# Bringing a layer's results back from features to token rows: TensorE transposes in place of 32x32 transposes and DMA moves

## The chip, the core and the metric

The kernel runs on one core of a Trainium2 chip. The metric is the device time of one execution in microseconds (us); of the kernel before, the median of three runs is 629.09 us.

## The reference

A linear attention without a softmax is followed by a two-level mixture of experts. Each of 4608 tokens (8 batches of 576) has 512 features (8 heads of 64).

```python
kv = np.einsum('bhsd,bhse->bhde', k, v)
out = np.einsum('bhsd,bhde->bhse', q, kv)
rms = np.sqrt(np.mean(out * out, axis=-1, keepdims=True) + 1e-06)
x = out / rms * g_norm            # then heads side by side: (4608, 512)
# each token: best of 4 groups, then best of that group's 4 experts, with softmax weights g_w, e_w
h = np.maximum(x[tokens] @ w1[g, e], 0.0)      # 512 -> 1024
out[tokens] = (g_w * e_w)[:, None] * (h @ w2[g, e])   # 1024 -> 512
```

## The kernel before

**Stages.** The first part (to about 150 us) computes the attention, the norms and the routing, writes each token's row with its factors into a DRAM scratch `scr`, and sorts the tokens by expert. Then the sixteen experts are worked off from the fullest to the emptiest. The list `CAPS` (line 22) gives each rank a fixed number of token places, 384 down to 256; what does not fit goes to an overflow loop at the end. Rank 0 has two of its three blocks done in the first part; its last block of 128 tokens is done at the start of the expert stage. Ranks 1 to 15 are the loop at line 1376.

**Precision.** A float32 operand is split into a high part in a rounded format (`whi`, `xh`, `hh`; ScalarE, lines 242, 1266, 280) and the rest (`wlo`, `xl`, `hl`; VectorE, lines 243, 1267, 281). A product is then three matmuls, high by high, high by rest and rest by high (`three`, lines 306, 307, 311).

**One rank r of the loop, of capacity `cap`.** Layer 1 runs over the eight chunks f of the hidden features: four times three matmuls into a bank `ps`, then ReLU and split into `hh` and `hl`. Layer 2 (`layer2_by_feature`, ranks 1 to 14) runs over the four chunks d of 128 output features: eight times three matmuls into one of three banks `psy`, with features in partitions and the rank's tokens side by side. Rank 15 uses `layer2_by_token`, which gives token rows at once. Besides, in layer 1 the weights of layer 2 are split by quarters (`split_piece`), and in layer 2 those of the next rank's layer 1; that is done by `side`, which also turns and splits the next rank's inputs.

**How inputs are turned.** The tokens' rows are gathered from `scr` (GpSimd, line 249) into `xg`, scaled by GpSimd, and written to a second scratch `xd` (`put_x`, line 1248). `get_x` (line 1254) reads them back as `xq`, so that a 32x32 transpose on VectorE (`turn_x`, line 1260) gives `xt` with features in partitions.

**How results go back.** Before the change VectorE transposes each `psy` bank in 32x32 squares into `yq` (line 1303, one buffer), and `move_y` (line 1274) then puts the squares in place with sixteen DMAs per rank on SP's queue, from `yq` to `yo`. `scatter_rows` (line 253) sends the rows of `yo`, up to 128 at a time, to the output on GpSimd's queue. Since the squares mix the column order, the weights of layer 2 are split in a permuted order (lines 236 to 238), each quarter in two instructions on each engine.

**The clears.** `yq` is written for a multiple of 32 tokens, so the banks are read past `cap`; line 1359 therefore clears part of each `psy` bank, after the first inputs are split and before the last block of rank 0 uses the banks.

**What sets the order.** In the expert stage the order of instructions on each engine is the order of the code, and each engine and queue works in order. SP's queue issues the weight loads (1 MB each, `load_next`, line 209), `put_x`, `get_x` and the moves. Weight tiles share a ring of twelve buffers, so a load waits until the split has read the tile it replaces.

Of the kernel before, what the change touches and what calls it, by code (L numbers as in the profile page):

```python
# [9 lines left out]
F32 = mybir.dt.float32  # L10
# [4 lines left out]
ALU = mybir.AluOpType  # L15
# [6 lines left out]
CAPS = [384, 364, 354, 330, 326, 312, 302, 300, 292, 290, 284, 274, 268, 264, 260, 256]  # L22
# [33 lines left out]
def tile_linattn_moe(ctx: ExitStack, tc: tile.TileContext, qm, qt, k, v, router, w1, w2, out):  # L56
    nc = tc.nc
    P = 128
    B, H, S, D = BATCH, HEADS, SEQ, HEAD_DIM
    NTOK, DM = out.shape  # L60
# [14 lines left out]
    KC = DM // P  # L75
# [8 lines left out]
    RW = DM + H  # L84
# [138 lines left out]
        return parts[0:2], parts[2:4], load  # L223

    def quarter(w, p):
        part = w[p // 2]
        if part[1] is None:  # L230
            for i, nm in ((1, "whi"), (2, "wlo")):
                part[i] = big.tile(list(part[0].shape), F32R, name=nm, tag="w8")
        if part[0].shape[1] == KC:
            n = part[0].shape[2] // 2
            return [[x[:, :, p % 2 * n:(p % 2 + 1) * n] for x in part]]
        src = w[p % 2][0].rearrange("p f (a c i) -> p a f c i", a=2, i=32)
        dst = [x.rearrange("p f (c a i) -> p a f c i", c=2, i=32) for x in part[1:]]
        return [[src[:, a, :, p // 2 * 2:p // 2 * 2 + 2]] + [x[:, p % 2 * 2 + a] for x in dst] for a in range(2)]

    def split_piece(w, p):  # L240
        for x, hi, lo in quarter(w, p):
            nc.scalar.copy(out=hi, in_=x)  # L242
            nc.vector.tensor_tensor(out=lo, in0=x, in1=hi.bitcast(F32), op=ALU.subtract)  # L243

    def blocks(cap):
        return [(j, min(P, cap - j * P)) for j in range((cap + P - 1) // P)]
# [892 lines left out]
    with ExitStack() as ph:  # L1139
# [75 lines left out]
                yield  # L1215
            nc.sync.dma_start(ovt, tab)


        psys = [ps_q.tile([P, 512], F32, name=f"psy{i}", tag=f"psy{i}") for i in range(3)]

        def next_psy():
# [3 lines left out]

        def moves(cap):

            part = [slice(32 * i, 32 * i + 32) for i in range(4)]  # L1230
            return [(a, s_, part[a], part[s_], len(range(s_, (cap + 31) // 32, 4)))
                    for k in range(4) for s_ in range(4) for a in [(s_ + k) % 4]]

        def gather(r):
            xg = mp.tile([P, 3, RW], F32, name="xg")
# [10 lines left out]
        def put_x(r, g):  # L1246
            for j, rows in blocks(CAPS[r] + -CAPS[r] % 32):
                nc.sync.dma_start(xd[r % 2][j * P:j * P + rows, :], g[0][0:rows, j, 0:DM])

        def get_x(r):  # L1250
            n = (CAPS[r] + 31) // 32
            xq = mp.tile([P, 12, P], F32, name="xq", bufs=1)
            for a in range(4):
                nc.sync.dma_start(xq[32 * a:32 * a + 32, 0:n, :],
                                  xd[r % 2][0:32 * n, a * P:(a + 1) * P].rearrange("(b i) f -> i b f", i=32))
            return xq, mp.tile([P, KC, 384], F32, name="xt", bufs=1)

        def turn_x(r, xq, xt, c):
# [8 lines left out]
            nc.vector.scalar_tensor_tensor(out=xl, in0=x, scalar=g2[:, 0:1], in1=xh.bitcast(F32), op0=ALU.mult,  # L1267
                                           op1=ALU.subtract)

        def move_y(r, yq):  # L1270
            yo = mp.tile([P, 3 * DM], F32, name="yo3", tag="yo3").rearrange("p (j f) -> p j f", j=3)
            pq = yq.rearrange("p (j s) f -> p j s f", s=4)
            for a, s_, pa, ps_, n in moves(CAPS[r]):
                nc.sync.dma_start(yo[ps_, 0:n, a * P:(a + 1) * P], pq[pa, 0:n, s_, :])  # L1274
            return [(yo[:, j], rows, gidx[:, r, j:j + 1]) for j, rows in blocks(CAPS[r])]

        def layer2_by_token(r, w2, hh, hl, side):
            n = 0
            for j, rows in blocks(CAPS[r]):
                yo = mp.tile([P, DM], F32, name="yo", bufs=2)  # L1280
                js = slice(j * P, j * P + rows)
                for hf in range(2):
                    side(n, 2 * len(blocks(CAPS[r])), 0)
                    ps = next_psy()
                    o = ps[0:rows, 0:DM // 2]
                    layer2_half(o, w2, hf, hh[:, :, js], hl[:, :, js])
                    nc.scalar.copy(out=by_quarter(yo)[0:rows, :, 2 * hf:2 * hf + 2], in_=by_chunk(o))
                    side(n, 2 * len(blocks(CAPS[r])), 1)
                    n += 1
                scatter_rows(yo, rows, gidx[:, r, j:j + 1])  # L1290

        def layer2_by_feature(r, w2, hh, hl, side):
            cap = CAPS[r]
            n = (cap + 31) // 32
            yq = mp.tile([P, 12, P], F32, name="yq", bufs=1)
            for d in range(KC):
                side(d, KC, 0)
                ps = next_psy()
                cs = slice((d % 2) * P, (d % 2 + 1) * P)
                _, wh, wl = w2[d // 2]  # L1300
                three(ps[:, 0:cap], FC, lambda c: wh[:, c, cs], lambda c: wl[:, c, cs], lambda c: hh[:, c, 0:cap],
                      lambda c: hl[:, c, 0:cap])
                nc.vector.transpose(out=yq[:, 0:n, 32 * d:32 * d + 32],  # L1303
                                    in_=ps[:, 0:32 * n].rearrange("p (b i) -> p b i", i=32))
                side(d, KC, 1)
            return r, yq

        ph.enter_context(tc.manual_schedule(engines={mybir.EngineType.PE, mybir.EngineType.Activation,
                                                     mybir.EngineType.DVE, mybir.EngineType.Pool, SP}))

        w1c, w2c = st["ws"][0:2], st["ws"][2:4]
        xT = mp.tile([P, KC, P], F32, name="xT", bufs=1)
        hr = mp.tile([P, 12, P], F32, name="hr", tag="yq", bufs=1).rearrange("p c t -> p (c t)")
        xr, xs = (mp.tile([P, 3 * DM], F32, name=nm, tag="yo3")[:, 0:n] for nm, n in (("xr", RW), ("xs", DM)))
        gather_rows(xr, P, gidx[:, 0, 2:3])
        cur = gather(1)
        w1n, w2n, load_next = weight_loads(eidx[0:1, 1:2])
# [37 lines left out]
        for c in range(KC):  # L1355
            turn_x(1, xq, xt, c)
            split_x(1, cur, xt, c)
        for x in psys:
            nc.vector.memset(x[:, DM // 2:384], 0.0)
        yo = mp.tile([P, DM], F32, name="yo", bufs=2)  # L1360
        for hf in range(2):
            ps = next_psy()
            o = ps[:, 0:DM // 2]
# [7 lines left out]
            load_next(i)  # L1371
        w1_at = {0: 2, 1: 3}
        w2_at = {2: 0, 4: 1, 5: 2, 7: 3}
        todo, results = None, []
        tables = overflow_tables()
        for r in range(1, NE):
            cap = CAPS[r]
            _, xh, xl = cur
            hh = mp.tile([P, FC, 384], F32R, name="hh", bufs=1)
            hl = mp.tile([P, FC, 384], F32R, name="hl", tag="hl", bufs=1)  # L1380
            if nxt:
                xq, xt = get_x(r + 1)
            if todo:
                results = move_y(*todo)
            for f in range(FC):
                if f in w1_at:
                    split_piece(w1c, w1_at[f])
                if f in w2_at:
                    split_piece(w2c, w2_at[f])
                ps = ps_h.tile([P, 512], F32, name="ps")  # L1390
                layer1(ps[:, 0:cap], w1c, f, xh[:, :, 0:cap], xl[:, :, 0:cap])
                split_h(hh[:, f, 0:cap], hl[:, f, 0:cap], ps[:, 0:cap])
                if r > 1:
                    next(tables, None)
                    next(tables, None)
                if f == 0:
                    nxt2 = gather(r + 2) if r + 2 < NE else None
                if nxt2 and f == 1:
                    scale(r + 2, nxt2)
                    put_x(r + 2, nxt2)  # L1400
                if nxt and f in (3, 5):
                    load_next((f + 1) // 2)
                if f >= 5 and results:
                    scatter_rows(*results.pop(0))
                if f == FC - 1 and r + 1 == NE:
                    nc.gpsimd.drain()
# [142 lines left out]
```

## Time and profile before

| | |
|---|---|
| runs | 629.09, 622.66, 629.69 us; median 629.09 |
| the profiled execution | 625.29 us, span 623.6 us |
| mean granted TensorE clock | 0.954 |
| busy | TensorE 90%, weight loads 84%, VectorE 60%, ScalarE 43%, GpSimd 34% |
| DMA | 156.70 MB, mean 251 GB/s |
| HBM | read 117.74 MB, written 29.31 MB |

A profile is one execution. Busy time is the share of the span in which an engine works at something. In the view of waits, "PE psy L306 <- DVE yq L1303" means that TensorE's matmuls into `psy`, line 306, stood until VectorE's write of `yq`, line 1303, was done. In a timeline the brackets give the idle time just before an instruction and what ended it. In a table of windows the granted clock is the share of full speed that TensorE was given in that stretch.

### The profile page before, as it was taken

What the parts mean: (1) busy time and instruction counts of PE and PEld (TensorE: products, weight loads), DVE (VectorE), ACT (ScalarE), POOL (GpSimd) and SP (SyncE); (2) the same over time, 40 slices, a digit from 0 to 9 for tenths busy, and PEclk for the clock granted to TensorE, in tenths of its full rate; (3) what the DMA queues carried; (4) which work ended last, traced back from release to release, by engine and by line L of the source; (5) the groups of instructions that cost most, each with busy time, mean ns of one, the idle gap of its engine ahead of it and who ended that gap; (6) DMA issues with size and microseconds to landing.
All of it is one profiled execution on the core that took longest, in us unless ns stands there. A gap on an engine that the chain in (4) does not pass through costs nothing.

```text
span 623.6 us, 13421 instructions
## 1 busy us (share of the span) xinstructions
PE 562.0 (90%) x5181; PEld 521.1 (84%) x5199; DVE 375.3 (60%) x786; ACT 267.2 (43%) x534; POOL 210.3 (34%) x281
## 2 busy tenths in 40 slices
PE   8888869999499999999999998979898979898895
PEld 4666757587189999999999997979898979798895
DVE  4235895862527686777677674657566565658470
ACT  0355645612225344544455453534353435345360
POOL 4032323245226235243144343334334243411103
PEclk9898999999889999999999999979998979798999
DMA  8999995648867769596959595969687777859541
GB/s 297 388 410 359 379 376 190 227 164 263 284 200 253 214 190 313 165 344 172 309 148 353 160 336 183 306 195 286 207 281 261 216 277 204 312 145 354 128 136 68
DMA packets 76788, 156.70 MB, mean 251 GB/s; under 512 B 10194, under 2 KB 49442, under 8 KB 65714
## 3 DMA queue, kind: packets, MB, share of 16 engines
q1 hardware_dynamic: 68752, 133.66, 66.3%
q0 software_dynamic: 7824, 22.11, 10.0%
q8 instruction: 42, 0.69, 0.4%
q10 hardware_dynamic: 146, 0.04, 0.1%
q14 instruction: 24, 0.20, 0.1%
HBM read 117.74 MB, written 29.31 MB: 236 GB/s over the span
## 4 chain that ended last, share of the span: by engine, by line
DMA 37%; PE 36%; SPq 14%; DVE 7%; issue 5%; ACT 1%; POOL 0%; POOLq 0%; DVEq 0%
DMA xq<-xd 20%; SPq L1274 12%; DMA wr<-in_w_dram 7%; PE warm L368 4%; DMA yo<-yq 3%; PE ps L311 3%; PE ps L307 3%; PE ps L306 3%; PE psy L311 3%; PE psy L307 3%; PE ops L521 3%; PE psy L306 3%; PE l L295 2%; DVE wlo L243 2%; PE kps L474 2%
## 5 line engine op out<-in xcount | busy, mean ns | idle before, releaser
L243 DVE TENSOR_TENSOR wlo<-wr,whi 128x1024 fp32r<-128x1024 f32 (+1 forms) x180 | 156.2, 895 | 36.6 <-ACT whi L242 34.4
L306 PE MATMUL psy<-hh,whi 128*128 128x364 f32 (+13 forms) x448 | 141.3, 315 | 22.4 <-DVE yq L1303 22.4
L307 PE MATMUL ps<-xl,whi 128*128 128x364 f32 (+14 forms) x480 | 144.2, 300 | 1.3 <-DVE xl L1267 1.3
L306 PE MATMUL ps<-xh,whi 128*128 128x364 f32 (+14 forms) x480 | 144.1, 300 | 0.4 <-DVE hl L281 0.3
L311 PE MATMUL ps<-xh,wlo 128*128 128x364 f32 (+14 forms) x480 | 144.2, 300 | 0.0
L307 PE MATMUL psy<-hl,whi 128*128 128x364 f32 (+13 forms) x448 | 140.3, 313 | 0.0
L311 PE MATMUL psy<-hh,wlo 128*128 128x364 f32 (+13 forms) x448 | 140.2, 313 | 0.0
L242 ACT CAST whi<-wr 128x1024 fp32r<-128x1024 f32 (+1 forms) x180 | 129.8, 757 | 19.5 <-DMA wr<-in_w_dram 19.5
L253 POOL DMA_INDIRECT out_dram<-yo,gall x45 | 47.9, 1064 | 204.4 <-DMA xd<-xg 99.8
L306 PEld LDWEIGHTS psy<-hh,whi 128*128 128x128 f32 x448 | 89.8, 201 | 24.2 <-DVE yq L1303 24.2
L280 ACT ACTIVATE hh<-ps 128x364 fp32r<-128x364 f32 (+14 forms) x120 | 49.8, 419 | 99.4 <-PE ps L311 97.2
L307 PEld LDWEIGHTS ps<-xl,whi 128*128 128x128 f32 x480 | 90.5, 189 | 1.8 <-DVE xl L1267 1.8
L306 PEld LDWEIGHTS ps<-xh,whi 128*128 128x128 f32 x480 | 90.9, 189 | 0.8 <-DVE hl L281 0.8
L277 POOL TENSOR_TENSOR xg<-xg 128x256 f32<-128x256 f32 x82 | 59.9, 755 | 93.2 <-DMA xg<-scr,gall 93.1
L311 PEld LDWEIGHTS ps<-xh,wlo 128*128 128x128 f32 x480 | 90.6, 189 | 0.0
L307 PEld LDWEIGHTS psy<-hl,whi 128*128 128x128 f32 x448 | 89.9, 201 | 0.0
L311 PEld LDWEIGHTS psy<-hh,wlo 128*128 128x128 f32 x448 | 89.8, 200 | 0.0
L1266 ACT ACTIVATE xh<-xt,rw 128x364 fp32r<-128x364 f32 (+14 forms) x60 | 32.6, 543 | 118.3 <-DVE xt L1260 105.3
L281 DVE SCALAR_TENSOR_TENSOR hl<-ps,hh 128x364 fp32r<-128x364 f32 (+14 forms) x120 | 54.8, 463 | 39.5 <-ACT hh L280 36.4
L1303 DVE STREAM_TRANSPOSE yq<-psy 128x320 f32<-128x320 f32 (+3 forms) x56 | 28.4, 508 | 80.1 <-DMA yo<-yq 62.9
L249 POOL DMA_INDIRECT xg<-scr,gall x44 | 57.3, 1302 | 13.3 <-issue 13.1
L368 PE MATMUL warm<-wide_b,ones_b 128*128 128x512 bf16 x124 | 37.0, 428 | 4.1 <-POOL wide_b L102 2.2
(255 smaller groups left out, 588.3 us busy)
## 6 DMA issues: line engine op xcount, KB each, us to landing
wr<-in_w_dram SPq DMA_DIRECT2D x64, 1024.0 KB
scr<-xo SPq DMA_DIRECT2D x36, 256.0 KB
m_q<-in_qm_dram SPq DMA_DIRECT2D x8, 1024.0 KB
xd<-xg SPq DMA_DIRECT2D x32, 256.0 KB
m_k<-in_k_dram SPq DMA_DIRECT2D x7, 1024.0 KB
m_v<-in_v_dram SPq DMA_DIRECT2D x7, 1024.0 KB
yo<-yq SPq DMA_DIRECT2D x116, 48.0 KB
yo<-yq SPq DMA_DIRECT2D x108, 32.0 KB
```

The lines of the kernel that those rows point to most:

```text
L242: nc.scalar.copy(out=hi, in_=x)
L243: nc.vector.tensor_tensor(out=lo, in0=x, in1=hi.bitcast(F32), op=ALU.subtract)
L249: return nc.gpsimd.indirect_dma_start(out=xg[0:rows, 0:RW], out_offset=None, in_=src, in_offset=bass.IndirectOffsetOnAxis(ap=idx[0:rows, : ...
L253: sc = nc.gpsimd.indirect_dma_start(out=out, out_offset=bass.IndirectOffsetOnAxis(ap=idx[0:rows, :], axis=0), in_=yo[0:rows, :], in_offset ...
L277: eng.tensor_tensor(out=out_[:, hs], in0=x[:, hs], in1=factors(xg)[:, h], op=ALU.mult)
L280: nc.scalar.activation(out=hh, in_=ps, func=AF.Relu)
L281: nc.vector.scalar_tensor_tensor(out=hl, in0=ps, scalar=0.0, in1=hh.bitcast(F32), op0=ALU.max, op1=ALU.subtract)
L306: nc.tensor.matmul(ps, lhsT=stat_h(c), rhs=mov_h(c), start=(c == 0), stop=False)
L307: nc.tensor.matmul(ps, lhsT=stat_h(c), rhs=mov_l(c), start=False, stop=False)
L311: nc.tensor.matmul(ps, lhsT=stat_l(d), rhs=mov_h(d), start=False, stop=(d == n - 1))
L368: nc.tensor.matmul(st["warm"], lhsT=ones_b, rhs=wide_b, start=True, stop=True)
L1274: nc.sync.dma_start(yo[ps_, 0:n, a * P:(a + 1) * P], pq[pa, 0:n, s_, :])
```

## The change

Inputs still take the way through `xd`. Results no longer pass through `yq` and the moves: ScalarE copies each `psy` bank to `yt` with its features in partitions (one buffer, as `yq` was); in the next rank's layer 1, after the chunks f = 1, 2 and 3, `back` transposes one block of 128 tokens each with four TensorE instructions into a bank `tp`, VectorE copies the bank to `yo`, and the rows are scattered. Ranks 1 to 14 have three blocks each. `yo` has four buffers of one block in place of two of three. The permuted split of the layer-2 weights becomes a plain one, with one instruction per quarter and engine, and a quarter now comes from one half of the weights where it came from both in turn. The clears are gone. `put_x` moves from f = 1 to f = 4, behind one weight load.

```diff
     def quarter(w, p):
...
-        if part[0].shape[1] == KC:
-            n = part[0].shape[2] // 2
-            return [[x[:, :, p % 2 * n:(p % 2 + 1) * n] for x in part]]
-        src = w[p % 2][0].rearrange("p f (a c i) -> p a f c i", a=2, i=32)
-        dst = [x.rearrange("p f (c a i) -> p a f c i", c=2, i=32) for x in part[1:]]
-        return [[src[:, a, :, p // 2 * 2:p // 2 * 2 + 2]] + [x[:, p % 2 * 2 + a] for x in dst] for a in range(2)]
+        n = part[0].shape[2] // 2
+        return [x[:, :, p % 2 * n:(p % 2 + 1) * n] for x in part]
...
-        def move_y(r, yq):
-            yo = mp.tile([P, 3 * DM], F32, name="yo3", tag="yo3").rearrange("p (j f) -> p j f", j=3)
-            pq = yq.rearrange("p (j s) f -> p j s f", s=4)
-            for a, s_, pa, ps_, n in moves(CAPS[r]):
-                nc.sync.dma_start(yo[ps_, 0:n, a * P:(a + 1) * P], pq[pa, 0:n, s_, :])
-            return [(yo[:, j], rows, gidx[:, r, j:j + 1]) for j, rows in blocks(CAPS[r])]
+        def back(r, yt, j, rows):
+            tp = ps_t.tile([P, 512], F32, name="tp2", tag="pst")
+            for d in range(KC):
+                nc.tensor.transpose(tp[0:rows, d * P:(d + 1) * P], yt[:, d, j * P:j * P + rows], ident)
+            yo = mp.tile([P, DM], F32, name="yo", bufs=4)
+            nc.vector.tensor_copy(out=yo[0:rows], in_=tp[0:rows, :])
+            scatter_rows(yo, rows, gidx[:, r, j:j + 1])
...
         def layer2_by_token(r, w2, hh, hl, side):
...
-                    nc.scalar.copy(out=by_quarter(yo)[0:rows, :, 2 * hf:2 * hf + 2], in_=by_chunk(o))
+                    nc.scalar.copy(out=yo[0:rows, hf * (DM // 2):(hf + 1) * (DM // 2)], in_=o)
...
         def layer2_by_feature(r, w2, hh, hl, side):
...
-            yq = mp.tile([P, 12, P], F32, name="yq", bufs=1)
+            yt = mp.tile([P, KC, 384], F32, name="yt", bufs=1)
...
-                nc.vector.transpose(out=yq[:, 0:n, 32 * d:32 * d + 32],
-                                    in_=ps[:, 0:32 * n].rearrange("p (b i) -> p b i", i=32))
+                nc.scalar.copy(out=yt[:, d, 0:cap], in_=ps[:, 0:cap])
                 side(d, KC, 1)
-            return r, yq
+            return [(r, yt, j, rows) for j, rows in blocks(cap)]
...
-        for x in psys:
-            nc.vector.memset(x[:, DM // 2:384], 0.0)
...
-            if todo:
-                results = move_y(*todo)
...
                 if nxt2 and f == 1:
                     scale(r + 2, nxt2)
-                    put_x(r + 2, nxt2)
                 if nxt and f in (3, 5):
                     load_next((f + 1) // 2)
-                if f >= 5 and results:
-                    scatter_rows(*results.pop(0))
+                if nxt2 and f == 4:
+                    put_x(r + 2, nxt2)
+                if f >= 1 and todo:
+                    back(*todo.pop(0))
```

Three places show how the instructions now stand. The first is VectorE at the start of the expert stage, where the inputs of rank 1 are turned and split and the `psy` banks were cleared; before:

```order
L1260 STREAM_TRANSPOSE xt<-xq 128x384
L1267 SCALAR_TENSOR_TENSOR xl<-xt,rw,xh 128x364
L1359 MEMSET psy_2443 128x128
L1359 MEMSET psy_2444 128x128
L1359 MEMSET psy_2442 128x128
L243 TENSOR_TENSOR wlo<-wr_2463,whi 128x4x256
```

and now:

```order
L1250 STREAM_TRANSPOSE xt<-xq 128x384
L1257 SCALAR_TENSOR_TENSOR xl<-xt,rw,xh 128x364
L237 TENSOR_TENSOR wlo<-wr_2463,whi 128x4x256
L275 SCALAR_TENSOR_TENSOR hl<-ps,hh 128x364
L237 TENSOR_TENSOR wlo<-wr_2463,whi 128x4x256
```

The three clears are gone; nothing else moves there. The second place is SP's queue around one `get_x` late in the loop (`wr` are weight loads, `xd` the rows of `put_x`); before:

```order
L1254 DMA xq<-xd_59 32x9x128 x4
L1274 DMA yo_5568<-yq 32x3x128 x2
L1274 DMA yo_5568<-yq 32x2x128 x2
L1274 DMA yo_5568<-yq 32x3x128 x2
L1274 DMA yo_5568<-yq 32x2x128 x2
L1274 DMA yo_5568<-yq 32x3x128 x2
L1274 DMA yo_5568<-yq 32x2x128 x2
L1274 DMA yo_5568<-yq 32x3x128 x2
L1274 DMA yo_5568<-yq 32x2x128 x2
L1248 DMA xd_58<-xg 128x512 x2
L1248 DMA xd_58<-xg 32x512
L209 ISA
```

and now:

```order
L1245 DMA xq<-xd_59 32x9x128 x4
L209 ISA
L209 DMA wr_5623<-in_w_dram 128x2048
L1239 DMA xd_58<-xg 128x512 x2
L1239 DMA xd_58<-xg 32x512
L209 ISA
L209 DMA wr_5672<-in_w_dram 128x2048
```

The sixteen moves are gone, and the rows for `xd` stand between the two weight loads instead of ahead of them. The third place is VectorE in layer 1 of the rank of capacity 284; before:

```order
L243 TENSOR_TENSOR wlo<-wr_5345,whi 128x16x32 x2
L281 SCALAR_TENSOR_TENSOR hl<-ps,hh 128x284 x2
L243 TENSOR_TENSOR wlo<-wr_5383,whi 128x16x32 x2
L281 SCALAR_TENSOR_TENSOR hl<-ps,hh 128x284 x2
L243 TENSOR_TENSOR wlo<-wr_5345,whi 128x16x32 x2
```

and now:

```order
L237 TENSOR_TENSOR wlo<-wr_5302,whi 128x8x128
L275 SCALAR_TENSOR_TENSOR hl<-ps,hh 128x284 x2
L1265 COPY yo<-tp_5571 128x512
L237 TENSOR_TENSOR wlo<-wr_5302,whi 128x8x128
L275 SCALAR_TENSOR_TENSOR hl<-ps,hh 128x284
L1265 COPY yo<-tp_5598 128x512
L275 SCALAR_TENSOR_TENSOR hl<-ps,hh 128x284
L1265 COPY yo<-tp_5625 34x512
L237 TENSOR_TENSOR wlo<-wr_5351,whi 128x8x128
```

Three copies come in between the `hl` of f = 1 to 3, and each weight split is one instruction where it was two. On TensorE each copy's four transposes stand right after the twelve matmuls of the same f.

More of the change, by code (lines that the diff above doesn't have):

```diff
@@ L232, in quarter @@
                 part[i] = big.tile(list(part[0].shape), F32R, name=nm, tag="w8")
-        if part[0].shape[1] == KC:
-            n = part[0].shape[2] // 2
-            return [[x[:, :, p % 2 * n:(p % 2 + 1) * n] for x in part]]
-        src = w[p % 2][0].rearrange("p f (a c i) -> p a f c i", a=2, i=32)
-        dst = [x.rearrange("p f (c a i) -> p a f c i", c=2, i=32) for x in part[1:]]
-        return [[src[:, a, :, p // 2 * 2:p // 2 * 2 + 2]] + [x[:, p % 2 * 2 + a] for x in dst] for a in range(2)]
+        n = part[0].shape[2] // 2
+        return [x[:, :, p % 2 * n:(p % 2 + 1) * n] for x in part]
     def split_piece(w, p):
-        for x, hi, lo in quarter(w, p):
-            nc.scalar.copy(out=hi, in_=x)
-            nc.vector.tensor_tensor(out=lo, in0=x, in1=hi.bitcast(F32), op=ALU.subtract)
+        x, hi, lo = quarter(w, p)
+        nc.scalar.copy(out=hi, in_=x)
+        nc.vector.tensor_tensor(out=lo, in0=x, in1=hi.bitcast(F32), op=ALU.subtract)
     def blocks(cap):
@@ L1223, in next_psy, with quarter_rows @@
             return psys[-1]
[L1228 to L1232, printed above, removed]
+        def quarter_rows(x, cap, a):
+            n = (cap + 31) // 32
+            return x[0:32 * n, a * P:(a + 1) * P].rearrange("(b i) f -> i b f", i=32)
         def gather(r):
@@ L1253, in get_x @@
             for a in range(4):
-                nc.sync.dma_start(xq[32 * a:32 * a + 32, 0:n, :],
-                                  xd[r % 2][0:32 * n, a * P:(a + 1) * P].rearrange("(b i) f -> i b f", i=32))
+                nc.sync.dma_start(xq[32 * a:32 * a + 32, 0:n, :], quarter_rows(xd[r % 2], CAPS[r], a))
             return xq, mp.tile([P, KC, 384], F32, name="xt", bufs=1)
@@ L1279, in layer2_by_token @@
             for j, rows in blocks(CAPS[r]):
-                yo = mp.tile([P, DM], F32, name="yo", bufs=2)
+                yo = mp.tile([P, DM], F32, name="yo", bufs=4)
                 js = slice(j * P, j * P + rows)
@@ L1293, in layer2_by_feature @@
             cap = CAPS[r]
-            n = (cap + 31) // 32
-            yq = mp.tile([P, 12, P], F32, name="yq", bufs=1)
+            yt = mp.tile([P, KC, 384], F32, name="yt", bufs=1)
             for d in range(KC):
@@ L1312, in tile_linattn_moe @@
         xT = mp.tile([P, KC, P], F32, name="xT", bufs=1)
-        hr = mp.tile([P, 12, P], F32, name="hr", tag="yq", bufs=1).rearrange("p c t -> p (c t)")
-        xr, xs = (mp.tile([P, 3 * DM], F32, name=nm, tag="yo3")[:, 0:n] for nm, n in (("xr", RW), ("xs", DM)))
+        hr = mp.tile([P, 12, P], F32, name="hr", tag="yt", bufs=1).rearrange("p c t -> p (c t)")
+        xr = mp.tile([P, RW], F32, name="xr", bufs=1)
+        xs = mp.tile([P, DM], F32, name="xs", tag="yo", bufs=4)
         gather_rows(xr, P, gidx[:, 0, 2:3])
@@ L1357, in tile_linattn_moe @@
             split_x(1, cur, xt, c)
-        for x in psys:
-            nc.vector.memset(x[:, DM // 2:384], 0.0)
-        yo = mp.tile([P, DM], F32, name="yo", bufs=2)
+        yo = mp.tile([P, DM], F32, name="yo", bufs=4)
         for hf in range(2):
@@ L1373, in tile_linattn_moe @@
         w2_at = {2: 0, 4: 1, 5: 2, 7: 3}
-        todo, results = None, []
+        todo = []
         tables = overflow_tables()
```

## The prediction

> **What bounds the kernel now.** I began with the page: busy shares and the forty slices.
>
> ```profile
> PE 562.0 (90%) x5181; PEld 521.1 (84%) x5199; DVE 375.3 (60%) x786; ACT 267.2 (43%) x534; POOL 210.3 (34%) x281
> ...
> PEclk9898999999889999999999999979998979798999
> ```
>
> TensorE is nearly always busy, so its gaps and its clock are the time that can be won, and its new instructions are the time that can be lost. The clock falls in single slices of the second half. The view of waits says what the gaps are (us in total, times, longest):
>
> ```profile
> PE psy L306 <- DVE yq L1303: 22.4, 8, 4.2
> PE psy L299 <- DVE psy L1359: 10.3, 1, 10.3
> ...
> PE ps L307 <- DVE xl L1267: 1.3, 2, 0.7
> ```
> ```profile
> DVE yq L1303 <- DMA yo<-yq: 62.9, 10, 7.6
> ```
>
> In eight experts TensorE waits for VectorE to empty a psy bank into `yq`, 22.4 us in all; VectorE had waited there for the moves that still read the one `yq` buffer. The timeline of one such round (SP's queue, VectorE, TensorE):
>
> ```profile
> 454.60 16.92 SPq L1274 DMA_DIRECT2D yo<-yq  x16
> ```
> ```profile
> 473.21 0.48 DVE L1303 STREAM_TRANSPOSE yq<-psy 128x288 f32<-128x288 f32 x1 [7.26 <-DMA yo<-yq]
> ```
> ```profile
> 473.75 0.40 PE L306 MATMUL psy<-hh,whi 128*128 128x284 f32 x1 [2.28 <-DVE yq L1303]
> 473.98 0.29 PE L307 MATMUL psy<-hl,whi 128*128 128x284 f32 x1
> 474.11 0.29 PE L311 MATMUL psy<-hh,wlo 128*128 128x284 f32 x1
> ...
> 474.89 0.44 PE L307 MATMUL psy<-hl,whi 128*128 128x284 f32 x1
> 475.13 0.44 PE L311 MATMUL psy<-hh,wlo 128*128 128x284 f32 x1
> ...
> 478.13 0.29 PE L306 MATMUL psy<-hh,whi 128*128 128x284 f32 x1
> ```
>
> SP issues sixteen moves over 16.9 us; VectorE stands 7.26 us, TensorE 2.28 us. Then comes a second price: matmuls start 0.13 us apart at first, 0.24 us apart from 474.89, and only at 478.13 are they fast again. The windows (core time; busy of PE, PEld, DVE, ACT, POOL; granted clock; DMA share; GB/s) show that for the rounds:
>
> ```profile
> 308.00:339.00 31.00, 31.00 (x221) 31.00 (x220) 22.10 (x37) 15.72 (x30) 11.94 (x13) 1.00 0.78 243
> ...
> 399.00:428.00 29.00, 25.18 (x168) 24.95 (x167) 15.89 (x29) 11.20 (x21) 11.67 (x13) 0.88 0.77 240
> 428.00:457.00 29.00, 26.51 (x195) 26.04 (x194) 18.39 (x32) 12.93 (x25) 12.55 (x12) 1.00 0.76 235
> 457.00:486.00 29.00, 26.72 (x194) 26.49 (x193) 18.59 (x34) 13.08 (x25) 11.10 (x12) 0.94 0.79 259
> 486.00:514.00 28.00, 23.81 (x173) 23.60 (x172) 15.75 (x28) 10.32 (x19) 11.79 (x12) 0.88 0.74 227
> 514.00:542.00 28.00, 25.03 (x180) 24.81 (x180) 15.94 (x28) 11.68 (x22) 11.39 (x11) 0.88 0.76 239
> 542.00:570.00 28.00, 24.65 (x188) 24.02 (x187) 17.43 (x32) 13.28 (x27) 5.40 (x7) 0.94 0.74 233
> 570.00:598.00 28.00, 26.18 (x207) 25.97 (x206) 18.47 (x35) 13.33 (x27) 2.97 (x3) 0.94 0.71 228
> ```
>
> At 308 to 339, with large capacities, TensorE is busy throughout at clock 1.00: the moves fit under the longer matmuls. From about 370 on the matmuls are shorter than the chain of moves, and the gaps begin.
>
> **The change, part by part.**
>
> *The moves go.* With no moves reading it, the buffer (now `yt`) is written by ScalarE at the end of each chunk of layer 2 and read by TensorE during f = 1 to 3 of the next layer 1, some eight matmul groups before it is written again. So the stall has no cause left: 22.4 us go, and the 1.3 us that TensorE waited for a late `xl`, which stood behind the `yq` transpose on VectorE. Half clock costs (1 - clock) times the window: 0.12 x 29 = 3.5, then 0, 0.06 x 29 = 1.7, 0.12 x 28 = 3.4, again 3.4, 0.06 x 28 = 1.7 and 1.7: 15.4 us. Together 39.1 us, in the profiled execution.
>
> *Clearing the banks goes.* The start of the expert stage:
>
> ```profile
> 139.73 9.44 PE L299 MATMUL l<-wr,h 128*128 128x256 f32 x43
> ...
> 152.47 0.60 PE L1334 MATMUL tp<-ident,xs 128*128 128x128 f32 x4
> 152.90 1.46 PE L299 MATMUL psy<-wr,h 128*128 128x256 f32 x6
> ...
> 172.90 9.51 PE L299 MATMUL psy<-wr,hT 128*128 128x256 f32 x32 [10.33 <-DVE psy L1359]
> 182.05 0.52 PE L306 MATMUL ps<-xh,whi 128*128 128x364 f32 x1
> ```
> ```profile
> 162.61 0.69 DVE L1346 COPY hT<-ps 128x512 f32<-128x512 f32 x1 [0.21 <-PE ps L1345]
> ...
> 172.06 0.60 DVE L1267 SCALAR_TENSOR_TENSOR xl<-xt,rw,xh 128x364 fp32r<-128x364 f32 x1 [0.67 <-ACT xh L1266]
> 172.68 0.45 DVE L1359 MEMSET psy<- 128x128 f32 x3
> ```
> ```profile
> 172.00:183.00 11.00, 10.10 (x37) 8.63 (x38) 1.04 (x4) 0.95 (x4) 0.00 (x0) 0.74 0.82 235
> ```
>
> The three clears cost 0.45 us themselves, but stand on VectorE behind the four `xl`, which wait for `xq`. TensorE needs only `hT`, there at 163.3. Without the clears its 32 matmuls run from 163.4 at the pace of the same matmuls at full clock, 9.44 / 43 = 0.22 us: 7.0 us, to 170.4. The next stage needs the last `xl` (172.66) only at its tenth matmul, some 1.6 us in: it loses about 0.6 us, and stands where it now would have begun at 171.0 in place of 182.05: 11 us. ScalarE's weight split, now held up by copies that wait for these matmuls, moves forward as well. The other end of this term is nothing, if later transfers hold the first rounds where they are.
>
> *TensorE's transposes come.* Fourteen experts, each with three blocks of four: 42 fours. Row 152.47 has four of the same shape and kind between two matmul groups; the next begins 0.43 us later. 42 x 0.43 = 18.1 us, all on the bounding engine, hidden by nothing. The third block is narrow; were its fours free, 28 x 0.43 = 12 us would be left, the lower end; the upper is 42 x 0.60 = 25 us, the whole length of row 152.47.
>
> *Copies and splits change engine or shape.*
>
> ```profile
> L242 ACT CAST whi<-wr 128x512 fp32r<-128x512 f32 x120 | 68.1, 617 | 19.5 <-DMA wr<-in_w_dram 19.5
> L242 ACT CAST whi<-wr 128x1024 fp32r<-128x1024 f32 x60 | 62.2, 1036 | 0.0
> ```
> ```profile
> L243 DVE TENSOR_TENSOR wlo<-wr,whi 128x512 fp32r<-128x512 f32 x120 | 81.0, 716 | 10.5 <-ACT whi L242 9.5
> L243 DVE TENSOR_TENSOR wlo<-wr,whi 128x1024 fp32r<-128x1024 f32 x60 | 75.1, 1252 | 26.1 <-ACT whi L242 24.9 <-DMA yo<-yq 0.5 <-issue 0.4
> ```
> ```profile
> L280 ACT ACTIVATE hh<-ps 128x364 fp32r<-128x364 f32 (+14 forms) x120 | 49.8, 419 | 99.4 <-PE ps L311 97.2
> L281 DVE SCALAR_TENSOR_TENSOR hl<-ps,hh 128x364 fp32r<-128x364 f32 (+14 forms) x120 | 54.8, 463 | 39.5 <-ACT hh L280 36.4
> ```
>
> Per expert ScalarE gains four copies of about 0.42 us (as `hh`, same width from PSUM) and saves 4 x (2 x 0.617 - 1.036) = 0.8 us: +0.9 on a busy 13 of 28. VectorE loses four transposes of about 0.5, gains three copies of 0.69 (the `hT` row, same shape), and saves 4 x (2 x 0.716 - 1.252) = 0.7. Its densest part is layer 1: 4 x 1.25 + 8 x 0.46 + 3 x 0.69 = 10.8 us, against eight groups of twelve matmuls (0.13 us each) plus three fours, 12.5 + 1.3 = 13.8 us. So both stay under TensorE, and I cost them at nothing; if that cover went, at the smallest capacity, the difference would be below 1 us an expert.
>
> *SP's queue is reordered.* The `xd` rows now stand behind one weight load, at f = 4. They wait for GpSimd's scaling anyway, and are read a whole expert later; behind them stands the second weight load, which waits for a split at f = 6. No cost.
>
> **Sum.** 625.3 (the profiled execution: 623.6 span and 1.7 around it) - 39.1 - 11.0 + 18.1 = 593.3 us. The median of the three runs is 3.8 above this execution; stalls and clock drops probably differ from run to run, and most of them go, so I add not 3.8 but 2: **595 us**.
>
> **Rivals.**
>
> *The start gains nothing* (first rounds held by transfers): 606 us. For it: DMA share 0.82 at 172 to 183. Against: with every load of that stretch already issued, TensorE filled the window 308 to 339 without a gap.
>
> *Transfers become the bound.* A round needs at most 0.76 x 29 = 22 us of DMA, moves included; the forecast's shortest rounds are about 24. Against it, then, but with little room: if weights held the last seven rounds for 1.7 us each, 607 us.
>
> *The transposes cool TensorE.* The Trainium skill's page "TensorE: Matmul & The Clock Gate", section "Part 4: PE-mode transpose", says that transposes don't count as activity for the clock gate. By it, three fours in a layer 1 could act like a gap. As a mechanism of this kernel: a half-clock stretch per expert at the price of the one above, 474.89 to 478.13, 3.2 us at half speed, is 1.6 us; 14 x 1.6 = 22 us, 617 us. Against: the round 428 to 457 had idle time (26.51 busy of 29) and kept clock 1.00; 0.43 us at a time is far shorter than the 2.28 us that cost the clock.
>
> *Slower: the result buffers bind.* Each copy into `yo` takes one of four buffers and waits for the scatter four copies back; VectorE stands still meanwhile, and behind the copy wait the weight splits and `hl`, for which TensorE waits. The scatters stand on GpSimd behind the gather and the scaling:
>
> ```profile
> 449.09 1.38 POOL L249 DMA_INDIRECT xg<-scr,gall  x1 [0.31 <-issue]
> ...
> 458.69 1.20 POOL L277 TENSOR_TENSOR xg<-xg 128x256 f32<-128x256 f32 x2 [4.68 <-DMA xg<-scr,gall]
> ...
> 462.81 1.20 POOL L277 TENSOR_TENSOR xg<-xg 128x256 f32<-128x256 f32 x2 [0.59 <-DMA xg<-scr,gall]
> ```
>
> Gather to end of scaling takes 15 us, three scatters some 3.5 more: 18 to 19 of a round of 24 to 26, so the buffer is free in time. It decides from 2.3 us of delay per expert (the 32 us forecast over 14). At the price of today's stall, 39.1 / 8 = 4.9 us, in all fourteen experts: 595 + 69 = 664 us; in the eight alone 634.
>
> **How the numbers follow.** Forecast 0.77; start without gain 0.08; transfers 0.08; cooling 0.03; buffers 0.04. The range is 584 to 608: below, cheap transposes (6 us less) and a median without the added 2 and a little more; above, either of the first two rivals, or dear transposes with some new small wait. It leaves out some 2 in 10 with the unnamed. Faster by over 2% (about what a measurement of this kernel can tell from no change), under 616.5 us: 0.93, the forecast and the first two. Within 2%: 0.05, cooling and the buffers in the eight. Slower: 0.02.
>
> **What would show it.** Right: no wait of `psy` matmuls for an emptied bank; clock 1.00 in all windows from 172 to the last expert; fours of transposes 0.43 us long and nothing idle around them; the first 364-wide matmul near 171; SP's queue mostly empty. Wrong: TensorE waiting for `tp`, `yt` or `hl` in layer 1; ScalarE waiting for `wr` by more than the 19.5 us now; clock below 1 behind the fours; an unchanged end of the first stage.

## The result, and the profile after

| | before | after |
|---|---|---|
| median of the runs (range) | 627.07 us (622.66 to 629.69, 4 runs) | 591.2 us (589.69 to 593.52, 4 runs) |
| after to before, with its 95% interval | | 0.9438 (0.9369 to 0.9507) |
| the profiled execution, its span | 625.29, 623.6 us | 593.52, 591.8 us |
| mean granted TensorE clock | 0.954 | 0.986 |

The forecast was 595 us. The page of the changed kernel, engines and clock:

```profile
PE 565.8 (96%) x5367; PEld 525.3 (89%) x5367; DVE 378.8 (64%) x709; ACT 281.7 (48%) x530; POOL 229.8 (39%) x281
...
PEclk9988898999999999999999999999999999999999
```

TensorE does 186 more matmul records, is busy 96% of the span where it was 90%, and the single slices of 7 and 8 in the second half are gone. Its view of waits has no row for `psy` or `tp` in the loop of ranks 1 to 15, and this one for `xl`, where 1.3 us stood:

```profile
PE ps L301 <- DVE xl L1257: 0.2, 1, 0.2
```

The windows of the prediction's table, three of them:

```profile
172.00:183.00 11.00, 10.80 (x64) 10.55 (x65) 8.00 (x11) 7.33 (x12) 5.10 (x4) 1.00 1.07 333
...
486.00:514.00 28.00, 28.00 (x229) 27.92 (x228) 19.34 (x28) 15.32 (x27) 10.77 (x9) 1.00 0.79 269
514.00:542.00 28.00, 28.00 (x237) 27.92 (x237) 20.76 (x32) 15.79 (x28) 4.45 (x4) 1.00 0.75 229
```

In the two late rounds TensorE has no idle time, at clock 1.00; 486 to 514 holds 229 matmul records where it held 173. The start of the expert stage, on TensorE:

```profile
163.00 7.17 PE L293 MATMUL psy<-wr,hT 128*128 128x256 f32 x32
169.82 0.52 PE L300 MATMUL ps<-xh,whi 128*128 128x364 f32 x1
...
171.87 0.43 PE L300 MATMUL ps<-xh,whi 128*128 128x364 f32 x1 [0.20 <-ACT xh L1256]
```

The 10.33 us ahead of the 32 matmuls are gone, and they run in 6.8 us where they took 9.2: the first 364-wide matmul stands at 169.82 in place of 182.05. A four of transposes in a later layer 1:

```profile
411.57 0.60 PE L1263 MATMUL tp<-ident,yt 128*128 128x128 f32 x4
411.92 0.38 PE L300 MATMUL ps<-xh,whi 128*128 128x290 f32 x1
412.14 0.30 PE L301 MATMUL ps<-xl,whi 128*128 128x290 f32 x1
```

From 411.57 to 412.14 pass 0.57 us, where one matmul's step is 0.13: a four costs 0.44 us.

So the 31.8 us between the two profiled executions come from three places: up to the first 364-wide matmul 12.2 us, from there to the last matmul 18.7 us (434.4 to 415.7), after it 0.9 us (7.2 to 6.3). In the middle part 42 fours put in 42 x 0.44 = 18.5 us, so what TensorE had lost there by waits and half clock is 37.2 us.

### The profile page after: what moved, and what is told of

Read it like the earlier page. It is cut to its first block, busy times and chain, and to the rows that moved or that the text cites. A ratio compares the mean times of both kernels' runs of the same rounds, so it can differ in the third digit from the quotient of the medians.

```text
span 591.8 us, 13382 instructions
## 1 busy us (share of the span) xinstructions
PE 565.8 (96%) x5367; PEld 525.3 (89%) x5367; DVE 378.8 (64%) x709; ACT 281.7 (48%) x530; POOL 229.8 (39%) x281
## 4 chain that ended last, share of the span: by engine, by line
issue 41%; POOL 23%; PE 18%; DMA 15%; ACT 1%; POOLq 1%; DVE 1%; SPq 0%; ACTq 0%
POOL out_dram L247 11%; DMA xg<-scr,gall 10%; POOL xg L271 10%; PE ops L515 4%; PE kps L468 3%; PE warm L362 3%; PE l L289 2%; DMA m_v<-in_v_dram 2%; PE l L293 2%; POOL xg L243 2%; DMA ktail<-in_k_dram 1%; PE tps L479 1%; DMA xs<-scr,sidx 1%; PE psy L293 1%; PE ps L289 1%
## 5 line engine op out<-in xcount | busy, mean ns | idle before, releaser
L237 DVE TENSOR_TENSOR wlo<-wr,whi 128x1024 fp32r<-128x1024 f32 x120 | 151.4, 1261 | 60.6 <-ACT whi L236 58.1
L247 POOL DMA_INDIRECT out_dram<-yo,gall x45 | 65.3, 1452 | 219.2 <-DVE yo L1265 195.0
L300 PE MATMUL psy<-hh,whi 128*128 128x364 f32 (+13 forms) x448 | 135.0, 301 | 0.0
L301 PE MATMUL psy<-hl,whi 128*128 128x364 f32 (+13 forms) x448 | 135.0, 301 | 0.0
L236 ACT CAST whi<-wr 128x1024 fp32r<-128x1024 f32 x120 | 125.0, 1042 | 0.0
L301 PEld LDWEIGHTS psy<-hl,whi 128*128 128x128 f32 x448 | 84.4, 188 | 0.0
L271 POOL TENSOR_TENSOR xg<-xg 128x256 f32<-128x256 f32 x82 | 69.3, 872 | 25.5 <-DMA xg<-scr,gall 25.3
L1293 ACT COPY yt<-psy 128x364 f32<-128x364 f32 (+13 forms) x56 | 23.1, 412 | 84.7 <-PE psy L305 84.6
L243 POOL DMA_INDIRECT xg<-scr,gall x44 | 49.3, 1121 | 13.3 <-issue 13.1
L1257 DVE SCALAR_TENSOR_TENSOR xl<-xt,rw,xh 128x364 fp32r<-128x364 f32 (+14 forms) x60 | 33.4, 576 | 25.4 <-ACT xh L1256 25.4
```

What stands on the lines that cost most here:

```text
L243: return nc.gpsimd.indirect_dma_start(out=xg[0:rows, 0:RW], out_offset=None, in_=src, in_offset=bass.IndirectOffsetOnAxis(ap=idx[0:rows, : ...
L247: sc = nc.gpsimd.indirect_dma_start(out=out, out_offset=bass.IndirectOffsetOnAxis(ap=idx[0:rows, :], axis=0), in_=yo[0:rows, :], in_offset ...
L271: eng.tensor_tensor(out=out_[:, hs], in0=x[:, hs], in1=factors(xg)[:, h], op=ALU.mult)
L300: nc.tensor.matmul(ps, lhsT=stat_h(c), rhs=mov_h(c), start=(c == 0), stop=False)
L301: nc.tensor.matmul(ps, lhsT=stat_h(c), rhs=mov_l(c), start=False, stop=False)
```

## What the stall was: a reading of the chain

One view, which the prediction did not read, stands ahead of the experiments, because they can't be understood without it: the chain of work that ended last, of the kernel before, in the stretch 440 to 505 (start, us, what; first the shares by line):

```profile
by line: DMA xq<-xd 52.3%; SPq L1274 23.6%; DMA yo<-yq 9.2%; DVE wlo L243 5.3%; DVE yq L1303 3.5%; DVE xl L1267 2.4%; issue 2.4%; DVE xt L1260 2.3%; DVEq L1303 0.5%; SPq L1254 0.2%
...
448.18 15.84 DMA xq<-xd
464.04 0.58 SPq L1274
...
470.93 1.91 DMA yo<-yq
...
473.21 0.48 DVE yq L1303
473.69 0.39 DVE xl L1267
474.08 1.14 DVE wlo L243
475.21 0.75 DVE xt L1260 x2
475.96 0.36 DVE yq L1303
476.35 18.14 DMA xq<-xd
```

This is a circuit, and TensorE is not in it. The four reads of the next inputs (`xq`) are issued straight behind four weight loads of 1 MB each, and land only after 15.84 us; then the moves go out, 0.64 us apart, 6.9 us; the last lands after 1.9; VectorE writes `yq`, and after `xl`, `wlo` and `xt`, 3.5 us in all, releases the next reads: 28.2 us in this round. Why the moves wait for the reads, and not for the buffer alone, is in the program. The order of SP's queue with its waits, one round (here of the version with two `yq` buffers below, where the buffer is not waited for):

```
L209 DMA wr_6320<-in_w_dram 128x2048 [waits DMAHW5_49,PE_49]
...
L1254 DMA xq<-xd_58 32x9x128 x3
L1274 DMA yo_6543<-yq 32x3x128 [waits DMASW7_49,DMASW6_49,DMAHW5_49,DMASW0_49,DVE_49]
L1274 DMA yo_6543<-yq 32x2x128 [waits DMAHW6_49]
L1274 DMA yo_6543<-yq 32x2x128 [waits DMAHW7_49]
L1274 DMA yo_6543<-yq 32x2x128 [waits DMAHW0_49]
L1274 DMA yo_6543<-yq 32x3x128 [waits DMAHW1_49]
```

Eight semaphores go round on SP's queue, and each transfer waits until the one eight places ahead of it has landed: the first four moves for the four weight loads, the next four for the four reads, the others for earlier moves.

## The experiments

The question was not whether the change gains, but whether it gains by what the prediction named. Its account: the moves hold the one `yq` buffer, VectorE waits for it, and the half clock that follows is a price of its own; the clears cost by their place behind the inputs; a four costs 0.43 us. Rivals: the moves cost by the place that they take in SP's queue; the half clock costs nothing while something else sets the round; the gain at the start comes from the clearing itself. The kernel before ran again beside each version, at medians of 622.5 to 627.9 us; ratios are to it, with the 95% interval. The changed kernel did not, so a difference to its 591.2 us is no surer than those 5 us.

**The clears back into the changed kernel**, at their old place:

```diff
+        for x in psys:
+            nc.vector.memset(x[:, DM // 2:384], 0.0)
```

> The changed kernel with the clears put back in their old place, behind the four input splits on VectorE. If their place was worth what the two profiles show (first 364-wide matmul at 169.8 in place of 182.05 us), about 603 us: 591 plus 12, TensorE idle some 10 us until VectorE's clears. If later transfers set the first rounds anyway (the rival), 591 to 595 us.

Measured 603.34 us, 0.9677 (0.9636 to 0.9719), 12 us above the changed kernel. TensorE:

```profile
171.09 9.26 PE L293 MATMUL psy<-wr,hT 128*128 128x256 f32 x32 [8.17 <-DVE psy L1349]
180.00 0.52 PE L300 MATMUL ps<-xh,whi 128*128 128x364 f32 x1
```

The wait is back, and so is the slow pace of the 32 matmuls behind it.

**The clears moved early in the kernel before**, ahead of the turning of rank 1's inputs; they are still done:

```diff
+        for x in psys:
+            nc.vector.memset(x[:, DM // 2:384], 0.0)
         for c in range(KC):
...
-        for x in psys:
-            nc.vector.memset(x[:, DM // 2:384], 0.0)
```

> The kernel before with the three clears moved ahead of the turning of rank 1's inputs on VectorE; nothing else changes. If waiting behind the inputs is the whole price of the clears, 615 us (627 minus 12) with the clears still done. If clearing itself or later transfers are the price, 625 to 627 us.

Measured 616.24 us, 0.9847 (0.9783 to 0.9911). TensorE's timeline, and its view of waits:

```profile
165.02 7.17 PE L299 MATMUL psy<-wr,hT 128*128 128x256 f32 x32 [0.97 <-DVE psy L1356]
171.84 0.52 PE L306 MATMUL ps<-xh,whi 128*128 128x364 f32 x1
```
```profile
PE psy L306 <- DVE yq L1303: 22.4, 8, 4.8
```

With the clearing done but not queued behind the inputs, the first 364-wide matmul stands at 171.84, 10.2 us earlier than before. The term is one of place on VectorE, and the stalls of the loop keep their 22.4 us: the two terms are separate.

**Two `yq` buffers in the kernel before.** Room for it comes from letting the small `yo` tiles share the large ones; the moves stay:

```diff
-            yq = mp.tile([P, 12, P], F32, name="yq", bufs=1)
+            yq = mp.tile([P, 12, P], F32, name="yq", bufs=2)
```

> The kernel before with two yq buffers in place of one (rank 0's last block and the last rank's rows take their yo from the yo3 buffers to make room); all moves and the clears stay. One-buffer theory: the stalls and the half-clock stretches go, 627 minus 39, 588 us, clock 1.00 from rank 2 on. Rival, the moves' own way through SP's queue and the DMA engines is the bound: the wait moves to the weights or the inputs, 610 to 627 us.

Measured 620.78 us, 0.9941 (0.9903 to 0.998). This is where the prediction's account of the stall falls. The waits, from the views of TensorE and ScalarE:

```profile
PE ps L306 <- DVE hl L281: 12.2, 4, 6.4
...
PE ps L306 <- DVE wlo L243: 7.2, 3, 3.2
```
```profile
ACT whi L242 <- DMA wr<-in_w_dram: 79.1, 18, 9.0
```

No `psy` matmul waits for `yq` any more, and TensorE waits for `hl` and for split weights instead: ScalarE, which writes `hh` and `whi` ahead of them, stands 79.1 us for weights, where it stood 19.5. The chain of this kernel, 470 to 512, and two rows of SP's timeline, the first loads of one round and of the next:

```profile
478.34 17.85 DMA xq<-xd
496.20 0.59 SPq L1274
...
504.19 0.59 SPq L1274
504.90 0.51 SPq L1248
...
509.73 15.90 DMA xq<-xd
```
```profile
475.67 2.49 SPq L209 DMA_DIRECT2D wr<-in_w_dram  x4
...
506.64 2.53 SPq L209 DMA_DIRECT2D wr<-in_w_dram  x4
```

The circuit has closed by another way. Where VectorE's 3.5 us led from the last move to the next reads, SP's own order now does: twelve moves behind the reads (8.6 us), then `xd`, the four loads and the reads again, 31.0 us in this round. From 424.03 to 545.85 SP's queue is taken for 118.7 of 121.8 us (sum of its sixteen groups, the waits inside them included). From the first layer-1 matmul of one rank to that of the next, the last eight rounds take 29.3 us on average, where they took 29.6.

**Both edits in the kernel before**, two buffers and early clears:

```diff
+            yq = mp.tile([P, 12, P], F32, name="yq", bufs=2)
...
+        for x in psys:
+            nc.vector.memset(x[:, DM // 2:384], 0.0)
         for c in range(KC):
```

> Both edits of the kernel before together: two yq buffers, clears ahead of the inputs. One-buffer theory: 627 minus 39 minus 12, 576 us, below the changed kernel, since no TensorE transposes are paid. Rival, SP's queue or DMA is the bound: 600 to 615 us.

Measured 610.69 us, 0.9777 (0.9732 to 0.9822). The two gains add, 1.5% and 0.6% to 2.2%, and 19 us to the changed kernel stay, though that one has 18 us of transposes on top.

**TensorE kept busy in the kernel before**: eight matmuls that nobody reads ahead of the last chunk of layer 2, in ranks 7 and up, so that the wait leaves no gap long enough to halve the clock:

```diff
+                if d == 3 and r >= 7:
+                    tp = ps_t.tile([P, 512], F32, name="tp", tag="pst")
+                    for _ in range(8):
+                        nc.tensor.matmul(tp, lhsT=ones_b, rhs=wide_b, start=True, stop=True)
```

> The kernel before with eight bf16 matmuls of 512 columns (about 1.8 us), whose result nobody reads, ahead of the last chunk of layer 2 from rank 7 on, where TensorE stands still anyway. Theory that the gap itself starts the half-clock stretches: gaps become 0 to 2.4 us, the clock stays near 1.00, and up to 15 us go: 610 to 615 us. Rival, SP's queue sets the length of a round whatever TensorE's clock: 622 to 630 us although the clock is better.

Measured 624.75 us, 1.0026 (0.9994 to 1.0059). Its profiled execution, of 629.7 us span, lies above that median, so only its clock and its idle times are read. In its other nine executions the mean clock has a median of 0.972, in the kernel before 0.961. A window, and TensorE's waits:

```profile
514.00:542.00 28.00, 25.87 (x196) 24.45 (x197) 17.19 (x31) 12.08 (x24) 12.03 (x13) 1.00 0.77 249
```
```profile
PE psy L306 <- DVE yq L1307: 12.0, 7, 2.5
```

The clock is 1.00 in this round where it was 0.88, and nothing is won. The filling itself takes about 1.7 us in each of eight ranks, 13.6 us, of which 10.4 lay in the wait for `yq` (22.4 to 12.0); the other 3 us are too few to hide the 15.4 us that the prediction gave to the clock. The half clock was not a price of its own: TensorE only used up slowly a time that the circuit gave it.

**Half of the moves on another queue**: both edits above, and every second move issued by ScalarE, two after each f of layer 1:

```diff
+                if i % 2 == 0:
+                    nc.sync.dma_start(yo[ps_, 0:n, a * P:(a + 1) * P], pq[pa, 0:n, s_, :])
+                else:
+                    late.append((yo[ps_, 0:n, a * P:(a + 1) * P], pq[pa, 0:n, s_, :]))
...
+                for _ in range(2 if late else 0):
+                    nc.scalar.dma_start(*late.pop(0))
```

> The kernel before with two yq buffers and early clears (610.7 us), and every other move issued from ScalarE's queue, two after each chunk f = 0 to 3. If the bound is the issue of sixteen moves one after another on SP's queue, half of them gone from it frees 5 us or more of each round: 575 to 590 us. If it is the transfer of the moves' bytes by the DMA engines, 605 to 615 us.

Measured 604.28 us, 0.9729 (0.9683 to 0.9774), 6.4 us better by the medians than both edits without it; the last eight rounds take 28.0 us on average in place of 29.2. What it gives back is seen on ScalarE's timeline and in TensorE's waits:

```profile
444.99 2.41 ACTq L1398 DMA_DIRECT2D yo<-yq  x2
447.44 0.41 ACT L280 ACTIVATE hh<-ps 128x284 fp32r<-128x284 f32 x1 [3.48 <-DMA yo<-yq]
```
```profile
PE ps L306 <- DVE hl L281: 24.2, 17, 3.5
```

ScalarE, held by its two moves, writes `hh` late, and TensorE waits 24.2 us for `hl` behind it. That the length of SP's queue counts is borne out; how much it is worth alone is not measured by this.

**Weights ahead of the moves**: both edits, with moves, `put_x` and scatters put behind both loads of layer-2 weights:

```diff
+                if nxt and todo and f == 6:
+                    results = move_y(*todo)
+                if nxt2 and f == 6:
+                    put_x(r + 2, nxt2)
```

> The kernel before with two yq buffers and early clears (610.7 us), and on SP's queue the moves and the xd rows set behind the two weight loads of layer 2 (at f = 6), their scatters behind layer 2. If the weights' place behind the moves was the remaining bound, the rounds fall to TensorE's own length: 574 to 585 us, below the changed kernel. If one queue cannot carry moves and loads in a round of 25 us, 595 to 612 us.

Measured 620.66 us, 0.9963 (0.9929 to 0.9997), 10 us worse than both edits. The waits of VectorE and of TensorE:

```profile
DVE xt L1260 <- DMA xq<-xd: 67.8, 10, 10.1
```
```profile
PE psy L306 <- DVE yq L1303: 27.7, 8, 4.5
```

Now the inputs come late, and VectorE, whose turning of them stands ahead of its `yq`, comes late to that: the wait is back by another way. In this order, too, a round has all the moves, loads and reads.

**The scatters a rank later**: early clears and three large `yo` buffers, so that no scatter waits for moves just issued:

```diff
+            due, results = results, move_y(*todo) if todo else []
...
+                if f >= (5 if nxt2 else 2) and due:
+                    scatter_rows(*due.pop(0))
```

> The kernel before with early clears (616 us), one yq buffer, three yo3 buffers in place of two, and each rank's result rows scattered one rank later, so that no scatter waits for moves at the head of GpSimd's queue and the next gather is not held behind it. Theory: a late round is a serial chain on the SP queue, loads 15 us (slowed by gathers and scatters that run just then), inputs 3.5, moves 10 at a third of the DMA engines, xd 2: 30 us. With gathers and scatters running during the moves the loads take some 4 us less: eight rounds, 580 to 597 us. If the chain does not depend on where the gathers and scatters run, 610 to 618 us.

Measured 613.03 us, 0.976 (0.9709 to 0.9811), which can't be told from the early clears alone (0.9783 to 0.9911). It did not do what it set out to: the scatters still wait for `xd`, which SP's queue sends behind the moves. GpSimd's timeline has

```profile
467.71 1.18 POOL L253 DMA_INDIRECT out_dram<-yo,gall  x1 [9.31 <-DMA xd<-xg]
```

just after that round's moves, as ever. What the run is good for is a row that the view of DMA issues shows (KB each, median us from issue to landing), here and in the changed kernel:

```profile
xq<-xd SPq DMA_DIRECT2D x20, 160.0 KB, 17.7
```
```profile
xq<-xd SPq DMA_DIRECT2D x20, 160.0 KB, 7.8
```

In the kernel with moves the reads take 17.7 us to land, in the changed one 7.8. That the moves make them slow is not shown by this; the third version below, with as many transfers on the queue, speaks against it.

**Sixteen transfers back on SP's queue of the changed kernel**, three versions. Per rank, sixteen transfers of the moves' sizes go into a tile `dead` that nobody reads. First from `xT`, which is never rewritten:

```diff
+            if r > 1:
+                for i in range(16):
+                    nc.sync.dma_start(dead[i % 4 * 32:i % 4 * 32 + 32, 0:CAPS[r - 1] // P + (i % 4 < 2), i // 4 * P:i // 4 * P + P],
+                                      xT[i // 4 * 32:i // 4 * 32 + 32, 0:CAPS[r - 1] // P + (i % 4 < 2), :])
```

> The changed kernel with sixteen DMAs of the old moves' shapes put back at their old place on SP's queue in ranks 2 to 15, from a constant tile to one nobody reads, so that no buffer waits for them. If the queue's occupation was the cause, the weights behind them come late, ScalarE waits for wr, TensorE stalls: 605 to 630 us. If only the yq buffer held by the moves was the cause, 591 to 595 us.

Second from `yt`, with two buffers of it, so that they wait for the end of layer 2 as the moves did; third the same with one buffer, which they then hold as the moves held `yq`:

```diff
-            yt = mp.tile([P, KC, 384], F32, name="yt", bufs=1)
+            yt = mp.tile([P, KC, 384], F32, name="yt", bufs=2)
...
+            if todo:
+                for i in range(16):
+                    a, s_ = i // 4, i % 4
+                    nc.sync.dma_start(dead[s_ * 32:s_ * 32 + 32, 0:2 + (s_ < 2), a * P:a * P + P],
+                                      todo[0][1][a * 32:a * 32 + 32, slice(1, 4) if s_ < 2 else slice(0, 4, 3), 0:P])
```

> As the run with dead moves, but the sixteen DMAs read yt, so that they cannot start before the last chunk of layer 2; yt has two buffers (small tiles share memory to make room), so that nobody waits for them. If moves that wait at the head of SP's queue for the end of layer 2 hold up the weights behind them, and that makes the stall: 600 to 620 us, ScalarE waiting for wr. If this wait is harmless as well: 591 to 597 us.

> The same dead moves from yt, with its one buffer, so that the next rank's copies into yt wait for them as the old transposes waited for the old moves. If holding the one buffer stalls TensorE by itself, more than the run with two yt buffers by 10 us or more, up to the 625 us of the kernel before plus the transposes. If the hold ends in time, the same as that run.

Measured 594.61 us, 0.9564 (0.9525 to 0.9603); 595.92 us, 0.9538 (0.9471 to 0.9605); 596.31 us, 0.9563 (0.9494 to 0.9632): 3 to 5 us over the changed kernel by the medians, no more than what the kernel before moves by from one time to the next. In the profiled executions of the first and the third, each of TensorE's rounds from rank 2 on is as long as in the changed kernel (32.4 us down to 24.4); holding the buffer adds nothing that can be measured. SP's queue and a window of the third:

```profile
489.12 15.41 SPq L1375 DMA_DIRECT2D dead<-yt  x16
504.78 0.38 SPq L209 DMA_DIRECT2D wr<-in_w_dram  x1
505.28 1.83 SPq L1239 DMA_DIRECT2D xd<-xg  x3
507.37 2.53 SPq L209 DMA_DIRECT2D wr<-in_w_dram  x3
512.61 2.35 SPq L1245 DMA_DIRECT2D xq<-xd  x4
515.00 16.05 SPq L1375 DMA_DIRECT2D dead<-yt  x16
...
531.31 0.37 SPq L209 DMA_DIRECT2D wr<-in_w_dram  x1
```
```profile
514.00:542.00 28.00, 28.00 (x237) 27.92 (x236) 19.49 (x31) 15.94 (x29) 4.39 (x3) 1.00 0.82 260
```

The sixteen take 13.4 to 16.1 us here, where the moves took 16.9 to 23.4 (kernel before and two buffers); from 425.03 to 541.69 the queue is taken for 96.4 of 116.7 us, and TensorE is never idle. So sixteen transfers on the queue, a wait at their head and one held buffer do not close the circuit by themselves. Two limits of this: the held buffer is written by ScalarE here, so the arc through VectorE to the next reads is not rebuilt, and the queue has little to spare, 26.5 us from the load at 504.78 to the one at 531.31. The reads land sooner with the same transfers around them: the fifth of the sixteen, which waits for the first read, goes out at 523.41, so that this read, issued at 512.61, took at most 10.8 us.

**The fours doubled in the changed kernel**, each block transposed twice into the same bank:

```diff
-            for d in range(KC):
+            for d in 2 * list(range(KC)):
```

> The changed kernel with every group of four transposes done twice into the same bank; the result is the same. If the transposes are paid in full on TensorE, some 0.36 us more for each of 42 groups, 15 us, up to 18: 606 to 609 us. If they fall into slack (the rival), 591 to 595 us. If transposes in a row cooled TensorE's clock, the granted clock would fall below 1.00 after rank 2 and the time pass 615 us.

Measured 612.17 us, 0.9822 (0.9782 to 0.9863), 21 us over the changed kernel. Every layer 1 grows by 1.31 to 1.39 us (of capacity 290: 14.16 to 15.55), 0.45 per four, 18.9 us in all; most of the rest is in rank 1. A window:

```profile
369.00:595.00 226.00, 226.00 (x1799) 224.80 (x1798) 155.85 (x225) 115.73 (x199) 81.98 (x78) 1.00 0.66 214
```

From 369 on, with 24 transposes in each layer 1, the clock is 1.00 throughout; a low clock of 0.84 at 172 to 183 lies ahead of the first of them.

No version was faster than the changed kernel.

## Why the prediction was right, and where its reasons were not

**The clears** (forecast 11.0, measured 12.2 us): right, mechanism and size. The 32 matmuls began 0.4 us earlier than forecast and took 6.8 us; TensorE then stood 0.4 us for the inputs (0.20 for `xh`, 0.20 for `xl`) where 0.6 was allowed. Both runs with displaced clears show the same wait come and go.

**The fours** (18.1, measured 18.5): right; 0.44 us each by the trace, 0.45 by doubling them. The narrow third block costs as much as the full ones: three fours make layer 1 about 1.3 us longer than layer 2 (capacity 290: 14.16 and 12.81 us).

**The moves** (39.1, measured 37.2): right in size, wrong in its reasons, at two steps.

The first is "VectorE had waited there for the moves that still read the one `yq` buffer ... So the stall has no cause left". The wait was there, but as one arc of a circuit whose long part is the 16 to 18 us in which weights and inputs land ahead of the moves on SP's queue. Two buffers cut that arc, and the late rounds went from 29.6 to 29.3 us. A second cause was left, the order of SP's queue itself. The change removes both, the wait for the moves and the moves. That taking them out is what gains is not shown, since sixteen transfers put back on the queue cost TensorE's rounds nothing in two of three versions; the plain split and the later `put_x` may have a part in it (see Open below).

The second is "Then comes a second price". With the clock at 1.00 in six of the eight late windows, in place of two, the kernel before was as slow (1.0026). The sum still came out, because behind the change TensorE is the bound: then all time in which it was idle or slow before is to be gained, under whatever name. The windows said how much, not why, so the number that came out is no test of these two steps.

**Costed at nothing.** ScalarE's copies and VectorE's copies of `tp`, the first on the page:

```profile
L1293 ACT COPY yt<-psy 128x364 f32<-128x364 f32 (+13 forms) x56 | 23.1, 412 | 84.7 <-PE psy L305 84.6
```

412 ns as allowed (0.42 us); VectorE's 42 copies of `tp` take 681 ns in the median, as allowed too (0.69), and TensorE waits for neither. The result buffers did not bind, nor did `put_x` at its later place. SP's queue is not the mostly empty one that the prediction expected; a late round there has

```profile
408.98 1.30 SPq L1239 DMA_DIRECT2D xd<-xg  x3
415.82 14.13 SPq L209 DMA_DIRECT2D wr<-in_w_dram  x3
430.13 2.14 SPq L1245 DMA_DIRECT2D xq<-xd  x4
```

where three loads take 14.13 us to go out, each when its tile is read; they are early enough, since TensorE waits for no weights.

**The rivals.** The start gained, and no transfer held a round. Cooling is refuted here: the fours, even doubled, left the clock at 1.00. The Trainium skill's page "TensorE: Matmul & The Clock Gate", section "Part 4: PE-mode transpose", has it that a transpose doesn't count as busy for the clock gate in the way that a matmul does; at 0.44 or 0.9 us between groups of twelve matmuls no run here shows an effect of that, and of longer stretches none shows anything.

**Open.** Why the same sixteen transfers close the circuit in the kernel before and not in the changed one. Three differences remain, and none was tried alone. In the kernel before and with two buffers `xd` goes out behind the moves and ahead of the loads, in the changed kernel behind the first load: from the end of the sixteen to the next load pass 1.9 us with two buffers (504.78 to 506.64) and 0.3 in the third version (531.05 to 531.31), in rounds of 31.0 and 26.5 us. The permuted split needs both halves of the layer-2 weights from the first chunk and frees them late, so that four loads go out at once ahead of the reads, where the plain split takes one half after the other; yet in the third version, too, the four go out within 5.1 us (504.78 to 509.90), against 2.5 with two buffers. And real results are scattered, so that gathers and scatters on GpSimd's queue run beside the weight loads. The chain of before has no GpSimd in it, which speaks against this last one; that is argued, not shown. TensorE itself needs 24.4 to 27 us a round behind the change, so a few us a round decide whether the queue holds it up.

## What to carry to other kernels

When TensorE waits, ask the chain of waits for the circuit that sets the round before naming a buffer: a second buffer cuts one arc, and the same queue can lead back by its own order. Here taking half of the moves off that queue helped by 6 us and another order of it did not; and whether the queue binds is a matter of a few us a round, as the versions with transfers put back show. The time that TensorE is idle or at half clock is the right measure of a gain only if TensorE is the bound afterwards. And a small instruction is dear by its place: three clears of 0.45 us together cost 12 us behind inputs for which the next matmuls had no need.

## What the hardware showed that was not expected

Small moves within the chip's memory were limited by their number: 0.64 us from one to the next on SP's queue, for 32 or 48 KB each, and about 1.9 us until the last had landed. Reads of 144 to 160 KB, issued behind four loads of 1 MB, took some 16 to 18 us to land, and 7.6 to 7.8 us (medians) in the changed kernel, where the loads go out one by one. With sixteen transfers a rank put back there, a read that was issued 2.7 us behind the last load had landed after at most 10.8 us, so many small moves by themselves don't make a read that slow.
